# Linear attention inside a mixture-of-experts kernel: transposed quadrant products, reciprocal by Ln and Exp, casting loads, and a new written order for the front

## The chip, the cores and the metric

The kernel runs on one core of a Trainium2 chip. The metric is device time in microseconds (us): 963.81 is the median of three runs of the kernel before. A profiled execution of it gives a trace of every instruction. PE is the matrix engine (TensorE), DVE is VectorE, ACT is ScalarE, POOL is GpSimd and SP is the engine that only issues DMAs.

## The reference

```python
# q, k, v: (8, 8, 576, 64) float32; phi(x) = elu(x) + 1
q_p, k_p = phi(q), phi(k)
kv  = einsum('bhsd,bhse->bhde', k_p, v)
z   = sum(k_p, axis=s)
num = einsum('bhsd,bhde->bhse', q_p, kv)
den = einsum('bhsd,bhd->bhs', q_p, z)[..., None] + 1e-06
x   = (num / den) transposed and reshaped to (4608, 512)
P   = exp(x @ w_gate - max), 8 rounds of row and column normalisation   # (4608, 8)
out = sum over 8 experts e of P[:, e] * (relu(x @ w1[e]) @ w2[e])       # w1: 512x1024, w2: 1024x512
```

Here `phi(x)` is written as min(exp(x), max(x + 1, 1)).

## The kernel before

The work has two stages that overlap. In the first, called the front here, 16 attention steps `att(b, g)` (batch b, four heads g, numbered n = 2b + g) turn q, k and v into the transposed activations `xT` (512 features by 4608 tokens, float16, in SBUF). In the second, 72 units (8 experts by 9 groups g of 512 tokens) each do a first layer and a second layer on PE. The first expert's units run between the attention steps, since unit g of expert 0 needs only the tokens 512g to 512g + 511, so unit 0 needs n = 0 and n = 1. The first five units of expert 0 are plain (`layer1`, L583, then the second layer, L809); all later ones use a seven-product scheme for 2x2 blocks (L703 and L927).

One attention step before: three loads of 576 KB (`kqin`, `vin`, float32, L269), exp of k and q on ACT (L285), max and min on DVE (L298, L301), a cast of v to float16 beside a column of ones (L229 on ACT or L231 on DVE), 18 products of 64 rows for k'v and z (`kv_ps`, L330), a copy that keeps the block diagonal (L341 or L343), nine transposes of q (`qt_ps`, L358), ten products for the denominator (`den_ps`, L373), a reciprocal on DVE (L379, L381), ten products for the numerator (`num_ps`, L397), a multiplication (L402), ten transposes to `xt_ps` (L413) and two copies to `xT`.

The loads of n = 0, 1 and 6 to 15 are issued by SP, those of n = 2 to 5 by POOL. POOL also issues the weights, which are cast from float32 to float16 on the way (L214), in halves for the first expert. At the start PE runs 47 products on zeros (`yw`, L505), which do no work of the kernel.

The order of the instructions on every engine is not the order of the Python loops. Each step is a task of `_Plan` (L18) with an engine, a planned duration, dependences, buffers to acquire and a priority. `run` (L52) goes through the planned time and emits the tasks: each engine takes, of the tasks that could start first, the one with the lowest priority number. A DMA is two tasks: the issue, on `sp` or `pool`, and its transfer, on one planned resource `dma`, which chooses by priority among the transfers already issued:

```python
ti = add(("pool", 1.0), fn, use=[g], prio=prio, deps=[tal, w_part.get(nm) if i else None])
ts_.append(add(("dma", 5.3 / parts), lambda _: None, deps=[ti], use=[g], prio=prio, lat=2.6))
```

The text `ranks` after the units overrides priorities of single tasks, and the engine of some. What is emitted is a fixed order per engine: on the chip an engine waits at each instruction until its operands are there, and does not take a later one first. From unit (1, 0) on the order on PE is fixed by `chain`.

`f_close` (L539) closes the front's buffers after the last attention step and opens those of the seven-product scheme; two products on zeros (`Zye`, L551) mark that place on PE.

Of the kernel before, what the change touches and what calls it, by code (L numbers as in the profile page):

```python
# [122 lines left out]
def kernel(  # L123
# [35 lines left out]
    aps = ctx.enter_context(tc.tile_pool(name="aps", bufs=2, space=PSUM))  # L159
# [5 lines left out]
    xT = xp.tile([P, NDT, N], FP16, tag="xT", name="xT")  # L165
    NXB = 7 * 512
    NL = 4
    NF = 8
    NX = 5
    MG = 99  # L170
# [11 lines left out]
    vv_t = [fp.tile([P, 2, NJ, D + 1], FP16, tag=f"vv{i}", name=f"vv{i}", bufs=1) for i in range(2)]  # L182
    kvps = front.enter_context(tc.tile_pool(name="kvps", bufs=1, space=PSUM))
    diag = fp.tile([P, 2, D + 1], FP16, tag="diag", name="diag", bufs=1)
    half_ = fp.tile([P, 2], FP32, tag="half", name="half", bufs=1)
    p_kv = S_.pool(1)

    p_in = {n: S_.pool(2) for n in "kvq"}
    p_e, p_t = S_.pool(2), S_.pool(2)
    p_vv, p_kvz, p_qpT, p_xn, p_rden = (S_.pool(2) for _ in range(5))  # L190
# [8 lines left out]
    def load_w(ten, nm, pl, ap, cut, e, prio, parts=1, after=0.0, deps=()):  # L199
# [6 lines left out]
        for i in range(parts):  # L206
            def fn(_, i=i):
                dst, a, off = g["tile"], [list(x) for x in ap], e * DM * F
                if parts > 1:
                    n = a[cut][1] // parts  # L210
                    off += i * n * a[cut][0]
                    a[cut][1] = n
                    dst = dst[:, i * n:(i + 1) * n, :] if cut == 1 else dst[:, :, i * n:(i + 1) * n]
                nc.gpsimd.dma_start(out=dst, in_=AP(tensor=ten.tensor, offset=off, ap=a))  # L214
            ti = add(("pool", 1.0), fn, use=[g], prio=prio, deps=[tal, w_part.get(nm) if i else None])
            w_part[nm] = ti
            ts_.append(add(("dma", 5.3 / parts), lambda _: None, deps=[ti], use=[g], prio=prio, lat=2.6))
            w_last[0] = ti
# [20 lines left out]
    v_land, kv_id = [], []  # L239
# [5 lines left out]

    def att(b, g):
# [3 lines left out]
        def ps_home(i):  # L250
            if n < 1 and i < 2:
                return p_ye[i], yps, f"ye{i}"
            return p_att, aps, "att"

        src = [[NJ * D, P], [2 * S * D, 2], [1, NJ * D]]
        gin, tin, gt, tph = {}, {}, {}, {}
        gkq = S_.grp(p_in["k"])
        for nm, ten in (("k", k), ("q", q), ("v", v)):
            gr = gin[nm] = S_.grp(p_in[nm]) if nm == "v" else gkq

            def fn(_, gr=gr, nm=nm, ten=ten):
                if nm == "v":
                    gr["tile"] = fp.tile([P, 2, NJ, D], FP32, tag="vin", name="vin", bufs=2)
                    dst = gr["tile"]
                else:
                    if nm == "k":
                        gr["tile"] = fp.tile([P, 2, 2, NJ, D], FP32, tag="kqin", name="kqin", bufs=2)
                    dst = gr["tile"][:, "kq".index(nm)]
                (nc.gpsimd if 2 <= n <= 5 else nc.sync).dma_start(  # L269
                    out=dst.rearrange("p r j d -> p r (j d)"),  # L270
                    in_=AP(tensor=ten.tensor, offset=(b * H + 4 * g) * S * D, ap=src))
            ti = fadd(("pool", 1.0) if 2 <= n <= 5 else ("sp", 0.45), fn, acq=[] if nm == "q" else [gr],
                      use=[gr] if nm == "q" else [], prio=pr,
                      deps=[w_last[0] if n in (2, 3, 4) else None, in_prev[0]])
            in_prev[0] = ti
            tin[nm] = fadd(("dma", 1.55), lambda _: None, deps=[ti], use=[gr], prio=pr, lat=2.6)
        ge, gtt = S_.grp(p_e), S_.grp(p_t)
        te = []
        for i, nm in enumerate("kq"):
            gt[nm] = gtt  # L280

            def f_e(_, i=i):
                if i == 0:
                    ge["tile"] = fp.tile([P, 2, 2, NJ, D], FP16, tag="e", name="e", bufs=2)
                nc.scalar.activation(out=ge["tile"][:, i], in_=gkq["tile"][:, i], func=AF.Exp)  # L285
            te.append(fadd(("act", 1.17), f_e, deps=[tin[nm], *te], acq=[] if i else [ge], use=[gkq, ge], prio=pr))
        tt_ = None
        for a0, a1 in ((0, 1), (1, 2)) if n < MG else ((0, 2),):
            def tv(g_, a0=a0, a1=a1):
                return g_["tile"][:, :, 2 * a0:2 * a1, :].rearrange("p j r d -> p r j d")  # L290

            def kv_in(g_, a0=a0, a1=a1):
                return g_["tile"][:, a0:a1].rearrange("p a r j d -> p (a r) j d")

            def f_t(_, a0=a0, tv=tv, kv_in=kv_in):
                if a0 == 0:
                    gtt["tile"] = fp.tile([P, NJ, 4, D], FP16, tag="t", name="t")
                nc.vector.tensor_scalar(out=tv(gtt), in0=kv_in(gkq), scalar1=1.0, scalar2=1.0, op0=ALU.add, op1=ALU.max)  # L298

            def f_m(_, tv=tv, kv_in=kv_in):  # L300
                nc.vector.tensor_tensor(out=tv(gtt), in0=tv(gtt), in1=kv_in(ge), op=ALU.min)  # L301
            w = a1 - a0
            tt_ = fadd(("dve", 0.77 if w == 1 else 1.36), f_t, deps=[tin[x] for x in "kq"[a0:a1]] + [tt_],
                       acq=[] if a0 else [gtt], use=[gkq, gtt], prio=pr)
            tm = fadd(("dve", 0.78 if w == 1 else 1.4), f_m, deps=[*te[a0:a1], tt_], use=[ge, gtt], prio=pr)
            for x in "kq"[a0:a1]:
                tph[x] = tm
        gvv = S_.grp(p_vv)
        tvv = []

        def f_va(_):
            gvv["tile"] = vv_t[(len(p_vv["order"]) - 1) % 2]
        ta = fadd(("none", 0.0), f_va, deps=[tin["v"]], acq=[gvv], prio=pr)
        def f_v(e):
            copy(e, gvv["tile"][:, :, :, 0:D], gin["v"]["tile"])
        tvv.append(fadd({"act": 1.15, "dve": 0.76}, f_v, deps=[ta, tin["v"]],
                        use=[gvv, gin["v"]], prio=pr))
        v_land.append(tin["v"])
        if n in (0, 15):
# [5 lines left out]
        def f_kv(_):  # L325
            gkv["tile"] = kvps.tile([P, 2, 512], FP32, tag="kv", name="kv_ps")
            for j in range(NJ):
                for hh in range(2):
                    s = slice(64 * hh, 64 * hh + 64)
                    nc.tensor.matmul(gkv["tile"][:, hh, 0:2 * (D + 1)].rearrange("p (r d) -> p r d", r=2),  # L330
                                     lhsT=gt["k"]["tile"][s, j, 0:2, :].rearrange("p r d -> p (r d)"),
                                     rhs=gvv["tile"][s, :, j, :], start=(j == 0), stop=(j == NJ - 1))
        kv_id.append(len(S_.t))
        tkv = fadd(("pe", 0.54), f_kv, deps=[tph["k"]] + tvv, acq=[gkv], use=[gvv, gt["k"]], prio=pr)

        def f_z(e):
            gz["tile"] = fp.tile([P, 2, 2, D + 1], FP16, tag="kvz", name="kvz")
            kv_ = gkv["tile"][:, :, 0:2 * (D + 1)].rearrange("p h (r d) -> p h r d", r=2)
            if e == "act":
                for r in range(2):  # L340
                    nc.scalar.mul(out=gz["tile"][:, :, r, :], in_=kv_[:, :, r, :], mul=half_[:, r:r + 1])  # L341
            else:
                nc.vector.tensor_tensor(out=gz["tile"], in0=kv_,  # L343
                                        in1=diag[:, None, :, :].broadcast_to([P, 2, 2, D + 1]), op=ALU.mult)
        tz = [fadd({"dve": 0.42, "act": 0.63}, f_z, deps=[tkv], acq=[gz], use=[gkv], prio=pr)]
        gq = S_.grp(p_qpT)

        def f_qa(_):
            gq["tile"] = fp.tile([P, 2, NJ, PW], FP16, tag="qpT", name="qpT")
        tqa = fadd(("none", 0.0), f_qa, deps=[tph["q"]], acq=[gq], prio=pr)  # L350
        tq = []
        for j0, j1 in ((0, 5), (5, NJ)):
            gp = S_.grp(p_att)

            def f_qt(_, j0=j0, j1=j1, gp=gp):
                gp["tile"] = aps.tile([P, 5, 2, PW], FP16, tag="att", name="qt_ps")
                for j in range(j0, j1):
                    nc.tensor.transpose(gp["tile"][:, j - j0, :, :].rearrange("p h w -> p (h w)"),  # L358
                                        gt["q"]["tile"][:, j, 2:4, :].rearrange("p r d -> p (r d)"), ident)

            def f_qc(e, j0=j0, j1=j1, gp=gp):
                copy(e, gq["tile"][:, :, j0:j1, :].rearrange("p h j w -> p j h w"), gp["tile"][:, 0:j1 - j0])
            t1 = fadd(("pe", 0.06 * (j1 - j0)), f_qt, deps=[tph["q"], tqa], acq=[gp], use=[gt["q"]], prio=pr)
            tq.append(fadd({"act": 0.165 + 0.105 * (j1 - j0), "dve": 0.14 + 0.069 * (j1 - j0)}, f_qc, deps=[t1, tqa],
# [836 lines left out]
```

## Time and profile before

| | us |
|---|---|
| runs of the kernel | 962.03, 963.81, 964.0 (median 963.81) |
| span of the profiled execution, first to last instruction | 960.4 |
| PE busy in it | 954.2 (99%) |
| DVE busy | 773.4 (81%) |
| ACT busy | 572.4 (60%) |
| POOL busy | 114.1 (12%) |

The median is 3.4 us above the span; the time around the span in that one execution is not recorded apart. The table counts a matmul as busy until its modelled end, and the products on zeros as busy too, so 99% does not mean that PE worked usefully all that time. The columns of the views below: in a chain, start, length and what it was; in a timeline, start, length, engine, source line, operation and tiles; in a group row, the count after x, then busy time and mean of one.

### The profile page before, as it was taken

How to read it: one execution, taken by the hardware profiler on the slowest of the kernel's cores; microseconds unless marked ns; L12 is line 12 of the kernel's file. 1: busy time of each engine (PE TensorE's matmuls, PEld its weight loads, DVE VectorE, ACT ScalarE, POOL GpSimd, SP SyncE). 2: the span in 40 equal slices, each digit the busy share in tenths (PEclk: the TensorE clock that was granted, in tenths of full speed). 3: DMA queues.
4: the chain of work that ended last, by engine and by line, in shares of the span. 5: the costliest groups of instructions: out<-in, count | busy, mean ns of one | idle time of the engine just before them, and what ended most of it. 6: DMA issues, size and time to landing. Idle time of an engine off the chain costs nothing.

```text
span 960.4 us, 21585 instructions
## 1 busy us (share of the span) xinstructions
PE 954.2 (99%) x8833; PEld 803.7 (84%) x8833; DVE 773.4 (81%) x1527; ACT 572.4 (60%) x1034; POOL 114.1 (12%) x163
## 2 busy tenths in 40 slices
PE   9999999999999999999999999999999999999998
PEld 4666676688888888888888888888888888888886
DVE  6998889878887888878887888878887888877775
ACT  6897755855555555555555555555555555555553
POOL 4100000011111111111111100111111111111110
PEclk9999999999999999999999999999999999999999
DMA  9987962252227222452227222272226321235554
GB/s 317 345 315 259 277 195 77 44 122 78 78 77 165 78 77 78 113 130 77 78 78 164 79 78 78 81 162 74 68 71 136 93 78 74 78 100 164 166 162 114
DMA packets 46420, 121.99 MB, mean 127 GB/s; under 512 B 4208, under 2 KB 18288, under 8 KB 46320
## 3 DMA queue, kind: packets, MB, share of 16 engines
q1 hardware_dynamic: 30576, 96.22, 30.1%
q0 software_dynamic: 15344, 23.87, 12.9%
q8 instruction: 69, 1.13, 0.5%
q10 hardware_dynamic: 400, 0.52, 0.2%
q14 instruction: 31, 0.25, 0.1%
HBM read 119.69 MB, written 17.69 MB: 143 GB/s over the span
## 4 chain that ended last, share of the span: by engine, by line
PE 95%; DMA 2%; ACT 2%; DVE 0%; issue 0%; POOL 0%; ACTq 0%; DVEq 0%
PE ye L927 34%; PE hq L703 24%; PE att L703 12%; PE ye L809 7%; PE Zye L703 6%; PE Zye L927 6%; PE hq L583 3%; DMA kqin<-in_k_dram 2%; ACT e L285 1%; PE xt_ps L413 1%; PE kv_ps L330 1%; PE num_ps L397 1%; PE qt_ps L358 1%; ACT h L587 0%; PE lg_ps L432 0%; PE den_ps L373 0%
## 5 line engine op out<-in xcount | busy, mean ns | idle before, releaser
L941 DVE SCALAR_TENSOR_TENSOR acc<-ye,P_sb,acc 128x256 f32<-128x256 f32 x620 | 267.3, 479 | 128.1 <-PE ye L927 127.6
L703 PEld LDWEIGHTS <-W 128*128 128x128 f16 x2144 | 209.8, 98 | 26.8 <-issue 0.2
L927 PEld LDWEIGHTS <-S 128*128 128x128 f16 x1984 | 194.1, 98 | 22.5
L927 PE MATMUL ye<-T,S 128*128 128x256 f16 x1488 | 192.8, 273 | 0.0
L703 PEld LDWEIGHTS <-w 128*128 128x128 f16 x1608 | 157.4, 98 | 20.1 <-issue 0.7
L735 ACT ACTIVATE h<-hq 128x512 f16<-128x512 f32 x134 | 80.1, 597 | 146.2 <-PE hq L703 143.3
L951 POOL TENSOR_TENSOR acc<-acc,st 128x256 f32<-128x256 f32 x124 | 87.3, 724 | 619.9 <-ACT st L948 609.2
L927 PEld LDWEIGHTS <-h 128*128 128x128 f16 x1488 | 145.6, 98 | 16.8
L703 PE MATMUL att<-xs,W 128*128 128x256 f16 x1008 | 151.2, 273 | 0.0
L703 PE MATMUL hq<-xs,W 128*128 128x256 f16 x1008 | 151.2, 273 | 0.0
L703 PE MATMUL hq<-xs,w 128*128 128x256 f16 x1008 | 140.9, 273 | 0.3 <-DVE h L738 0.3
L732 ACT ACTIVATE h<-Zye 128x512 f16<-128x512 f32 x134 | 80.1, 598 | 42.6 <-PE Zye L703 42.6
L948 ACT ACTIVATE st<-Zye,P_sb 128x256 f32<-128x256 f32 x124 | 51.9, 470 | 78.0 <-PE Zye L927 78.0
L900 DVE TENSOR_TENSOR S<-h 128x1024 f16<-128x1024 f16 x124 | 85.4, 689 | 13.7 <-ACT h L735 13.7
L738 DVE CUSTOM_DVE_ANT_0 h<-att,s 128x512 f16<-128x512 f32 x126 | 86.7, 688 | 11.7 <-ACT s L722 11.1
L722 ACT COPY s<-hq 128x512 f32<-128x512 f32 x126 | 73.6, 584 | 36.3 <-PE hq L703 36.3
L715 ACT COPY Zye<-hq 128x512 f32<-128x512 f32 x134 | 78.0, 582 | 17.8 <-PE hq L703 17.7
L738 DVE CUSTOM_DVE_ANT_0 h<-hq,s 128x512 f16<-128x512 f32 x126 | 86.7, 688 | 0.6 <-PE hq L703 0.6
L809 PE MATMUL ye<-w,h 128*128 128x512 f16 x312 | 76.6, 379 | 0.0
L703 PE MATMUL Zye<-xs,w 128*128 128x256 f16 x504 | 75.6, 273 | 0.0
L729 ACT COPY s<-att 128x512 f32<-128x512 f32 x126 | 74.6, 592 | 0.0
L927 PE MATMUL ye<-w,h 128*128 128x256 f16 x496 | 64.3, 273 | 0.0
(109 smaller groups left out, 949.7 us busy)
## 6 DMA issues: line engine op xcount, KB each, us to landing
xs<-xd SPq DMA_DIRECT2D x63, 896.0 KB, 4.6
w<-in_moe_w_dram POOLq DMA_DIRECT2D x14, 1024.0 KB, 11.5
out_dram<-acc SPq DMA_DIRECT2D x67, 128.0 KB, 2.4
kqin<-in_k_dram SPq DMA_DIRECT2D x12, 576.0 KB, 5.2
kqin<-in_q_dram SPq DMA_DIRECT2D x12, 576.0 KB, 6.6
vin<-in_v_dram SPq DMA_DIRECT2D x12, 576.0 KB, 7.3
xd<-acc SPq DMA_DIRECT2D x5, 512.0 KB, 4.9
kqin<-in_k_dram POOLq DMA_DIRECT2D x4, 576.0 KB, 10.5
```

The source lines that it names most:

```text
L703: nc.tensor.matmul(dst[:, p, :], lhsT=lhs(p, c), rhs=rhs(c), start=(first and p == 0 and c == 0), stop=(c == 1), skip_group_check=True)
L715: nc.scalar.copy(out=Zt[1], in_=gX["tile"])
L722: nc.scalar.copy(out=gs2["tile"], in_=gX["tile"])
L729: nc.scalar.copy(out=gs5["tile"], in_=gR["tile"])
L732: nc.scalar.activation(out=hd(0, 0), in_=Zt[1], func=AF.Relu)
L735: nc.scalar.activation(out=hd(1, 0), in_=gX["tile"], func=AF.Relu)
L738: nc.vector._custom_dve(TENSOR_ADD_SAT, out=dst, in0=ps, in1=sb, s0=3.0e38, s1=0.0)
L809: nc.tensor.matmul(gy[tt]["tile"], lhsT=gh["tile"][:, f, ds(P * tt, P)], rhs=gw2["tile"][:, f, :], start=(f == 0), stop=(f == NFT - 1))
L900: nc.vector.tensor_tensor(out=Sx[:, i], in0=a0, in1=a1, op=op)
L927: nc.tensor.matmul(bank(g_)[:, s, :], lhsT=lhs(s, kk), rhs=rhs(kk), start=(new and s == 0 and kk == 0), stop=(kk == 3), skip_group_check=True)
L941: nc.vector.scalar_tensor_tensor(out=dst(), in0=bank(g_)[:, s, :], scalar=P_sb[:, gg, e:e + 1], in1=dst(), op0=ALU.mult, op1=ALU.add)
L951: nc.gpsimd.tensor_tensor(out=dst(), in0=dst(), in1=gst["tile"], op=ALU.add)
```

## The change

The attention step is written anew, the loads are cast, and the order of the front is another.

1. q and v are loaded as float16 (`qin`, and `vv` with its ones column set once), k as float32 (`kin`), each with three buffers. All loads but the first k are issued by POOL, in one fixed sequence with the first expert's weights: n = 0, n = 1, both halves of w1, the first half of w2, n = 2, the second half of w2, n = 3, and so on. The weights no longer wait for the landing of the first v.
2. q is transposed before phi: 18 transposes of 128x64 blocks (L333 in the new file) into `at2`, one PSUM tile of two banks. Then exp on ACT (L337) and max and min on DVE (L340, L343) on the transposed q.
3. k'v has 192 columns (ones shared by two heads, L308). Numerator and denominator are made transposed, by 64x64 products over 288 tokens (`quads`, L359); the denominator is repeated over 64 rows by a broadcast operand.
4. 1/den is Exp(-Ln(den + 1e-6)) on ACT (L372 twice, L377). A multiplication on DVE writes `xT` (L387), so that the transposes of x and their copies are gone. The numerator uses the PSUM bank of `kv`.
5. The relu of `layer1` may go to ACT or DVE. The bank that was `aps` with two buffers is `at2` for all its users.
6. `ranks` is replaced by `order`, a new list of ranks for the tasks of the front.

```diff
-    vv_t = [fp.tile([P, 2, NJ, D + 1], FP16, tag=f"vv{i}", name=f"vv{i}", bufs=1) for i in range(2)]
+    vv_t = [fp.tile([P, 3, NJ, D], FP16, tag=f"vv{i}", name=f"vv{i}", bufs=1) for i in range(NV)]
...
-            ti = add(("pool", 1.0), fn, use=[g], prio=prio, deps=[tal, w_part.get(nm) if i else None])
+            ti = add(("pool", 0.85), fn, use=[g], prio=prio, deps=[tal, w_part.get(nm) if i else None] + ([in_prev[0]] if e == 0 else []))
+            if e == 0:
+                in_prev[0] = ti
+                if i == 0 and mid:
+                    mid()
...
+        def quads(dst, c, z):
+            for hh in range(2):
+                for r in range(2):
+                    s, o = slice(64 * r, 64 * r + 64), 64 * hh
+                    w = gz["tile"][s, hh, D * (1 - r):D * (1 - r) + 1].broadcast_to([64, D]) if z else gz["tile"][s, hh, r:r + D]
+                    nc.tensor.matmul(dst[o:o + 64, r, 0:CH], lhsT=w,
+                                     rhs=gq["tile"][s, hh, :, :].rearrange("p j w -> p (j w)")[:, CH * c:CH * c + CH],
+                                     start=True, stop=True)
...
+            t1 = fadd(("pe", 0.2), f_den, deps=[tq, *tz], acq=gd, use=[gq, gz], prio=pr)
+            tl.append(fadd(("act", 0.75), f_ln, deps=[t1, *tl], acq=[] if c else [grd], use=[*gd, grd], prio=pr))
+
+        def f_ex(_):
+            nc.scalar.activation(out=grd["tile"], in_=grd["tile"], func=AF.Exp, scale=-1.0)
...
+                nc.vector.tensor_tensor(out=xT[:, 2 * g:2 * g + 2, S * b + CH * c:S * b + CH * c + CH],
+                                        in0=gn["tile"][:, :, 0:CH], in1=grd["tile"][:, c], op=ALU.mult)
...
-    w_t = {0: load_w1(0, prio=-290.0, parts=2, deps=[gates[0]])}
-    for b in range(1, B):
+    w_t = {0: load_w1(0, prio=-290.0, parts=2)}
+    w_t[0] += load_w2(0, prio=-98.5, parts=2, mid=lambda: att(1, 0))
+    att(1, 1)
+    for b in range(2, B):
         att(b, 0)
         att(b, 1)
-        if b == 1:
-            w_t[0] += load_w2(0, prio=-96.5, parts=2, deps=[in_prev[0]])
...
-    ranks = """
+    order = """
...
-    for w in ranks.split():
-        n, p, *en = w.split(":")
+    for i, w in enumerate(order.split()):
+        n, *en = w.split(":")
         t = S_.t[int(n)]
-        t["prio"] = float(p)
-        if en and en[0] in t["eng"]:
+        t["prio"] = 0.1 * i - 2000.0
+        if en:
             t["eng"] = {en[0]: t["eng"][en[0]]}
```

The order that comes out of this for the first microseconds, engine by engine (the numbers of the attention steps are read from the loads' source offsets): POOL issues q0, v0, k1, q1, v1, w1 in two halves, half of w2, k2, q2, v2, the rest of w2, k3, q3, v3, k4, q4, v4. ACT does exp(k0), exp(q0), exp(q1), exp(k1), the two Ln and the Exp of n = 0, the two Ln of n = 1, exp(k3), then the Exp of n = 1 and exp(q3). DVE makes xT of the first half of n = 0, then max and min of k3, then xT of n = 1's first half and of n = 0's second half. PE does the transposes and k'v of n = 0 and 1, their denominators and three of their four numerators, then the transposes of q3, k'v of n = 3, and only then the first eight products of unit 0's first layer (L554).

## The prediction

> **What bounds the kernel now.** I read the busy windows first, then the chain in order of time, then the groups of PE, and last the landings of single loads.
>
> ```profile
> 20.00:34.30 14.30, 14.03 (x136) 7.98 (x136) 12.09 (x24) 10.90 (x17) 4.98 (x7) 1.00 1.15 326
> ...
> 39.30:126.00 86.70, 86.28 (x1010) 54.76 (x1011) 75.51 (x159) 70.62 (x112) 2.09 (x3) 1.00 0.89 285
> ```
>
> The columns are stretch, length, then busy time of PE, weight loads, DVE, ACT and POOL, clock, DMA share, GB/s. From 20 us on PE has almost no idle time; DVE is at 87% and ACT at 81% from 39 to 126. After 193 us PE steps from product to product without a gap. So the time is the end of the start-up plus PE's remaining work, and a microsecond without useful PE work is lost.
>
> The chain shows the start-up:
>
> ```profile
> 0.74 4.30 DMA kqin<-in_k_dram
> ...
> 10.19 9.44 DMA kqin<-in_k_dram
> ...
> 19.71 1.16 ACT e L285
> ...
> 38.67 0.62 PE kv_ps L330 x18
> ...
> 40.56 1.75 PE hq L583 x8
> ...
> 129.05 0.45 PE Zye L551 x2
> ```
>
> The first k lands at 5.04, k2 at 19.63 (10.19 + 9.44). Loads are the limit there. The single issues continue this: v1 issued at 3.53 took 9.0, landing at 12.5; w1's halves issued at 8.54 and 9.46 took 6.3 and 8.0 (14.9, 17.5); v2 issued at 11.97 took 10.7 (22.7); v3 at 14.74 took 12.3 (27.0); the last half of w2, issued at 17.79, took 14.4 (32.2). Landings follow the order of issue, 1.5 us for a load of 576 KB and about 2.5 for half a weight.
>
> What PE did meanwhile, in the groups of PE up to 39.3 us:
>
> ```profile
> L505 PE MATMUL yw<-warm 128*128 128x512 f16 x47 | 14.3, 437 | 1.3 <-DVE warm L493 1.3
> L583 PE MATMUL hq<-xT,w 128*128 128x512 f16 x32 | 7.9, 378 | 0.1
> L809 PE MATMUL ye<-w,h 128*128 128x512 f16 x28 | 7.2, 378 | 0.0
> ...
> L330 PE MATMUL kv_ps<-vv,t 64*128 64x130 f16 x90 | 3.5, 217 | 0.2 <-ACT vv L229 0.2
> L413 PE MATMUL xt_ps<-ident,xn 128*128 128x128 f16 x40 | 3.2, 219 | 0.0
> ```
>
> In the chain four 512-column products step in 0.86 us, so 32 + 28 are 12.9 us; five k'v groups at 0.62, 38 transposes of q and 40 of x at 0.06, 40 numerators at 0.058, 40 denominators at 0.025 add 3.1 + 4.7 + 2.3 + 1.0. Useful work by 39.3: about 24.0 us.
>
> **The change, start-up.** The new sequence of loads is k0, q0, v0, k1, q1, v1, w1, w1, half of w2, n = 2, half of w2, n = 3. That is what landed by 32.2 before (six loads, four halves, six loads), in another order. With v1 at 12.5 as before, three halves bring 20.1, n = 2 24.6, the last half 27.2, then k3 28.7 to 29.2, q3 1.5 later, v3 at 31.7 to 32.2. The casts of q and v are priced by the weights: float32 read at 1 MB in 2.5 us gives 1.4 to 1.5 for 576 KB. POOL's issues take 0.7 to 1.1 us each, less than a landing, and its waits (eight transfers outstanding, buffers of n = 0 and 1) end well before the queue runs dry.
>
> The instructions do not follow that order. ACT has exp(k3) ahead of the Exp of n = 1, DVE has max and min of k3 ahead of two of the first xT halves, and PE has the transposes of q3 and k'v of n = 3 ahead of layer 1 of unit 0, which itself needs neither. n = 2, landed seven microseconds earlier, comes later in all three. So everything waits for k3 and then v3. By hand: n = 0 and 1 are done by about 20 us but for the Exp of n = 1 and three multiplications. k3 at 29.2; exp(k3) to 30.4 (1.18); Exp of n = 1 to 31.6; xT of n = 1, first half, to 32.4 (0.75: the 512-element row of L402 is 0.69, its 256-element row 0.42); numerator and xT of n = 0, second half, to 33.4; k'v of n = 3, waiting for that bank and for v3, to 34.4. Layer 1 starts at 34.4, where before it began at 17.13 with two products and at 19.95 in bulk.
>
> Its first eight products end at 36.1. The next need the last half of n = 1, and DVE has before it exp(q3)'s partner max at 34.5 (exp(q3) ends at 34.45, and max waits for it), then six more of about 0.75, 0.75, 0.27, 0.74, 0.75, 0.74 and 0.75: 39.3. PE's useful work by 39.3 is then: three k'v at 0.92, three sets of q transposes at 0.61, ten groups of quadrant products at 0.18 (all three priced below) and eight layer-1 products, 1.7: 8.1 us. **Deficit 24.0 - 8.1 = 15.9 us.**
>
> **Attention on PE.** Before, one step costs 0.62 (k'v) + 0.61 (transposes of q) + 0.25 (den) + 0.58 (num) + 0.63 (transposes of x) = 2.69. After: k'v has 192 columns for 130; 0.62 x 192/130 = 0.92. The 18 products of 130 columns in 0.62 are 0.034 each, where full-height ones of 130 columns would be 0.055 (215 ns for 512), so 64-row products do run two side by side. For the 64-column half-width of the new transposes no row exists: 18 at half of 0.068 is 0.61, one after another 1.22. Sixteen quadrant products of 288 columns (0.121 each): four side by side 0.18 a group with its start, two side by side 0.24 or more. I take four, as rows of 64 already pair: 0.92 + 0.61 + 0.72 = 2.25, **a saving of 0.44 x 16 = 7.0 us**. Two side by side and serial transposes: 0.92 + 1.22 + 1.0 = 3.14, a loss of 7. Best case 0.75 + 0.5 + 0.55 = 1.8, a saving of 14.
>
> The Trainium skill, page "TensorEngine Tiling (Array Packing)", sections "Key Properties" and "Restrictions", speaks against this: a change of tiling mode drains the array, and column tiling gives up the fast weight load. In the trace the k'v groups, a mode of their own amid full-size products, show no drain that stands out in their 0.62 us; for columns no run here shows it.
>
> **Clock.** The first products on zeros start every 0.43 us up to 6.0 us, then 0.21, although the clock column says 1.00. PE now has little to do from 20 to 32 us, so it may be slow again: k'v of n = 3 on the path would cost 0.9 more, and what follows 39.3 up to the 2.3 that the first slow stretch lost (1.33 to 6.0 at half speed). I take 1.5, of 0 to 3. The page "TensorE: Matmul & The Clock Gate", Part 1, has the clock halve after an idle window of about 3.4 us and return after as much work; by that one such stretch would lose an estimated 1.7 us at most, and the sum would stand 0.2 higher.
>
> **ACT and DVE.** Before, one step is 11.5 us of both (exp 2.36, max and min 3.0, cast 1.1, kvz 0.6, copies 2.2, reciprocal 0.45, multiplication 1.8). After: exp of k 1.18, of q 1.17, two Ln 1.3, Exp 1.18, max and min 1.5 + 1.5, kvz 0.54, two multiplications 1.5: 9.9. Ln has no row; I price it as a 576-element copy from PSUM on ACT (0.65 in L229), between 0.6 and 0.9. The 1.6 x 16 = 25 us off two engines hide behind PE. But those engines stand idle from 20 to 29. From 29.2 on about 141 of attention, 25 of relus, 12 of second-layer copies and 8 of x blocks remain: 186 over two engines, 93 at full use, 111 at the 84% of the second window above. So the front closes between 122 and 140, while PE would need 39.3 + 70 (five plain units) - 1.7 + 16 x 2.25 - 6.4 + 3 = 140. They are close: 2 us of extra idle time, of -2 to +6. POOL adds to it: v5 is issued behind the release of v2's buffer, at about 47.
>
> **Everything else.** The relu on either engine and the ones column are free at this load. The steady units keep their order; the one PSUM tile adds a wait of PE for DVE ahead of one product group in 61 units. Before, that DVE step ends at 507.69 and the group starts at 507.92; a hop from DVE to PE takes 0.06, so 0.17 us covers it. Without that cover each 0.1 us would cost 6.
>
> **Sum.** +15.9 - 7.0 + 1.5 + 2 = +12.4. On the span: 972.8; on the median, 3.4 above the span: 976.2, taken as 976. With each term at its good end (14 saved, no clock loss, idle -2, v3 half a microsecond early) it is -1; at its bad end +15.9 + 7 + 3 + 6 = +32.
>
> **Rivals.** *Quadrants or half-width transposes run in pairs at best:* 3.14 a step, +27, about 990. For it: no row with 64 columns. Against: 64-row pairs do overlap.
> *PE saves more and the lighter ACT and DVE close gaps:* 1.85 a step saves 13.4, and with no extra idle time +15.9 - 13.4 + 1.5 = +4, about 968.
> *Not slower: v3 lands early.* If transfers of this all-POOL sequence overtake one another as the plan's ranks have it, layer 1 starts up to 13 us sooner, at about 21.5, bound by n = 1. Each microsecond earlier than 32.2 pays one; the break-even is v3 at about 20, and with v3 at 17 the whole is 12.4 - 12.9 - 1.5 (clock) - 2 (the second wait) = -4, 960. Against it: k2 behind both halves of w1, landing after them, and every later load in order of issue.
> *The steady units lose their 0.17 us of cover:* +6 or more on top, 982 and up.
>
> **How the numbers follow.** Forecast 0.62; pairs only 0.18; larger saving 0.12; early landing 0.05; steady units 0.03. The range 966 to 988 takes the forecast with its terms, the larger saving and the lower part of the pairs. About 0.2% (1.9 us) is what can be told from no change; faster by more is the early landing alone, 0.05, within it 0.03, slower 0.92.
>
> **What would show it.** Right: k3 landing near 29 and v3 near 32; exp(k3) as the longest wait of ACT, some 9 us; the first eight L554 products near 34 and the next near 39; the two products on zeros at the front's end near 140 for 129.05; from there on the distance to the end unchanged at 831 us. Wrong: L554 near 21, a quadrant group of 0.3 us or more, or the units after 200 us longer than 12.2 us.

## The result and the profile after

The changed kernel takes 990.25 us (median of 4 runs, 989.43 to 991.04) where the kernel before, on the same chip, took 963.9: a ratio of 1.0272, with a 95% interval of 1.0257 to 1.0287. The profiled execution has a span of 987.7 us. The sign of the forecast holds; the loss is 26 us where 12 were forecast, and 990 lies above the range.

The busy windows of the changed kernel (stretch, length, busy PE, weight loads, DVE, ACT, POOL, granted clock, DMA share, GB/s):

```profile
20.00:34.30 14.30, 3.29 (x41) 2.30 (x41) 3.04 (x4) 3.74 (x4) 4.35 (x6) 0.61 1.17 258
34.30:39.30 5.00, 4.13 (x29) 1.62 (x24) 4.75 (x8) 3.46 (x6) 0.00 (x0) 0.75 0.88 192
39.30:126.00 86.70, 82.18 (x838) 39.63 (x838) 60.32 (x99) 65.17 (x93) 23.36 (x31) 1.00 0.74 176
```

PE, which was busy for 14.03 of the first stretch, now is for 3.29, at a granted clock of 0.61. And from 39.3 on, where PE was to work almost without a break, it has 82.18 of 86.70, with *less* work on DVE and ACT than before.

The landing of k3 in the chain, the timeline of PE at the end of the start-up, and what was waited for from 18 to 60 us (total, times, longest):

```profile
13.01 15.61 DMA kin<-in_k_dram
28.61 0.02 issue
28.63 1.16 ACT ek L284
```

```profile
31.69 0.46 PE L359 MATMUL num_ps<-qpT,kvz 64*64 64x288 f16 x4 [11.01 <-DVE xT L387]
32.08 1.17 PE L333 MATMUL att<-ident,qin 128*64 128x128 f16 x18
33.19 1.62 PE L308 MATMUL kv_ps<-vv,t 64*128 64x192 f16 x18
34.74 2.89 PE L554 MATMUL hq<-xT,w 128*128 128x512 f16 x8
...
39.18 0.59 PE L554 MATMUL hq<-xT,w 128*128 128x512 f16 x2
```

```profile
POOL vv L272 <- PE kv_ps L308: 15.2, 1, 15.2
PE num_ps L359 <- DVE xT L387: 11.0, 1, 11.0
DVE t L288 <- DMA kin<-in_k_dram: 9.1, 1, 9.1
ACT ek L284 <- DMA kin<-in_k_dram: 8.1, 1, 8.1
```

This is the start-up that was traced by hand: ACT and DVE at k3, PE behind DVE, layer 1 at 34.74 and again at 39.18.

**Where PE's time went.** I sum, in both traces, from the start of each product to the start of the next. The plain step of its shape (215.5 ns for 512 columns, 109 for 256, in a row of small products what they take in the row) is work; if the tile shape changes between two products, up to 0.1 us of the excess is put down to that; the rest is waiting.

| us | zeros | work | changes of shape (number) | waiting | sum | close of the front |
|---|---|---|---|---|---|---|
| before | 13.0 | 933.8 | 2.9 (31) | 5.4 | 955.0 | 128.91 |
| after | 25.5 | 925.3 | 12.5 (130) | 18.8 | 982.1 | 153.42 |
| difference | +12.5 | -8.5 | +9.6 | +13.4 | +27.1 | +24.5 |

The numbers are rounded. The close is the start of the first product on zeros of `Zye`, here before and after (the 129.05 of the prediction is its place in the chain):

```profile
128.91 0.59 PE L551 MATMUL Zye<-warm 128*128 128x512 f16 x2
153.42 0.59 PE L522 MATMUL Zye<-warm 128*128 128x512 f16 x2
```

The column of zeros takes in what passes between a product on zeros and the next start: its +12.5 is for the most part PE standing idle up to 31.69, behind the last of these products. Of the waiting, 2.6 us lie between 31.7 and 39.3 (about 1 of them is the slow clock on the first eight products of layer 1), 9.0 between 39.3 and the close (before: 1.3), and 3.4 more than before after the close, around the column sums of the Sinkhorn rounds, for a reason that no run shows; later the units stand as before.

A change of shape can be read in the timeline, where four 512-column products ahead of quadrants take 0.95 us to the next start (56.68 to 57.63) and not 0.86:

```profile
56.68 1.02 PE L782 MATMUL ye<-w,h 128*128 128x512 f16 x4
57.63 0.32 PE L359 MATMUL num_ps<-qpT,kvz 64*64 64x288 f16 x4
57.88 1.90 PE L782 MATMUL ye<-w,h 128*128 128x512 f16 x8
```

Single starts say the same: 309 ns from a 512-column product to a quadrant, a 128x64 transpose or a k'v product, and about 0.1 us on the way back (239 ns from the start of a group's last quadrant to a 512-column product, 137 to the next group of quadrants). In the trace before only k'v did this (312 ns); transposes, numerators and denominators had full-size tiles and cost nothing (215 ns).

The waits of DVE after 39 us, and the chain there, show a second thing that the change brought:

```profile
DVE qpT L340 <- ACT eq L337: 14.0, 12, 2.4
```

```profile
45.63 1.14 ACT eq L337
...
46.80 0.77 DVE qpT L340
...
47.61 0.71 PE att L333 x18
48.34 1.14 ACT eq L337
...
49.50 0.77 DVE qpT L340
...
50.31 0.34 PE att L359 x4
50.65 0.02 issue
50.67 0.75 ACT rden L372
```

The max of q (L340) starts when the Exp (L337) has ended, one behind the other on the one PSUM tile `at2`; the denominators and the next step's transposes need that tile too. After 39 us the chain goes through such a pair nine times. Before, exp and max read SBUF and ran beside each other.

### The profile page after: what moved, and what is told of

Read it like the earlier page. It is cut to its first block, busy times and chain, and to the rows that moved or that the text cites. A ratio compares the mean times of both kernels' runs of the same rounds, so it can differ in the third digit from the quotient of the medians.

```text
span 987.7 us, 21380 instructions
## 1 busy us (share of the span) xinstructions
PE 961.1 (97%) x8753; PEld 789.0 (80%) x8753; DVE 765.5 (78%) x1463; ACT 574.1 (58%) x1022; POOL 139.2 (14%) x197
## 4 chain that ended last, share of the span: by engine, by line
PE 89%; DVE 4%; ACT 3%; DMA 2%; issue 1%; POOL 0%; POOLq 0%; ACTq 0%
PE ye L900 33%; PE hq L676 23%; PE att L676 12%; PE Zye L676 6%; PE Zye L900 5%; PE ye L782 5%; PE hq L554 3%; DMA kin<-in_k_dram 2%; ACT eq L337 1%; PE kv_ps L308 1%; PE att L333 1%; DVE qpT L340 1%; DMA vv<-in_v_dram 1%; PE num_ps L359 0%; ACT rden L377 0%
## 5 line engine op out<-in xcount | busy, mean ns | idle before, releaser
L900 PEld LDWEIGHTS <-S 128*128 128x128 f16 x1984 | 194.1, 98 | 22.5
```

The source lines that it names most:

```text
L900: nc.tensor.matmul(bank(g_)[:, s, :], lhsT=lhs(s, kk), rhs=rhs(kk), start=(new and s == 0 and kk == 0), stop=(kk == 3), skip_group_check=True)
```

## Experiments

The kernel before ran again beside each round of experiments, with medians of 963.1 to 964.1 us, so runs of different rounds can be compared to about 1 us.

My first theory was the start-up alone, with the written order as its cause: the plan lets its loads land by priority (k3 ahead of k2 and of half the weights), and the chip lands them as issued.

**The plan serves loads in order of issue (e1); the same without the written list (e2).**

```diff
-                    if r is not None and r <= te + 1e-9 and (pick is None or (t["prio"], t["id"]) < (pick["prio"], pick["id"])):
+                    if r is not None and r <= te + 1e-9 and (pick is None or key(t) < key(pick)):
     # key(t): (ready, id) for the transfers, else (prio, id); in e2 the text `order` is gone too
```

> The plan serves its loads in the order in which POOL issues them, as the chip did (k2 landed at 21.81, k3 at 28.61); the written list of ranks stays. Theory 'start-up only': the 26 us are the instructions that wait for n = 3; in the new order on PE both groups n = 0 and 1 and ten layer-1 products come ahead of anything of n = 2 and 3, so layer 1 starts near 21 for 34.74, the products on zeros keep PE from 20 to 31.7 no longer, and the front closes 24 us sooner, near 130; time about 965. Theory 'start-up and shape changes': layer 1 near 21 too, but only the first part comes back, 11.6 us of idle time and 3.8 of waits before 39.3; the 130 changes of tile shape (12.5 us) stay and the close is near 140; time about 976. Rival 'the list itself is at odds with the landings': ranks that were found for other landings give their gain back later, layer 1 near 21 and yet the close at 150 or later; time 985 or more.

> As the last one, and the written list is left out: every step has the rank of its group n, the lower first. Layer 1 needs n = 0 and 1 alone (v1 landed at 12.35) and starts near 20. Theory 'start-up only': close near 130 to 135, time 965 to 970. Theory 'start-up and shape changes': shape changes are as many as before (117 in the front, 0.095 us each), so close near 140, time 975 to 978. Rival 'the list is what costs': this one beats the kernel that keeps the list by 5 us or more. Rival 'nothing in the order matters': within 2 us of 990.

Measured: 1028.43 and 1000.34, both slower than 990. Layer 1 starts at 22.47 and 20.93 as expected, and the idle stretch is gone; but the close comes at 179.6 and 150.6, and PE's waiting is about 67 and 38 us. So a start-up that is 12 us shorter can be worth less than nothing: the rest of the front has to fit as well. "Start-up only" fell, and the rivals that put the cost on the written list held: with the right landings the plan is 28 us faster without it. But e2 too is 10 us slower than the changed kernel. I did not follow every wait in these two.

**The price of a change of shape, alone (z1, z2).**

```diff
                         nc.tensor.matmul(bank(g_)[:, s, :], lhsT=lhs(s, kk), rhs=rhs(kk),
                                          start=(new and s == 0 and kk == 0), stop=(kk == 3), skip_group_check=True)
+                        if s == 0 and kk == 1:   # z1: r = c = 128; z2: r = c = 64
+                            nc.tensor.matmul(bank(g_)[0:c, s, :], lhsT=warm[0:r, 0:c], rhs=warm[0:r, 0:256],
+                                             start=False, stop=False, skip_group_check=True)
```

> Measures the disputed cost by itself, in the steady units, where PE steps without a gap: after the second of the eight products of each of 434 groups one more product of 128x128 on zeros is added to the same bank (256 columns, adds nothing). Both theories: 434 x 0.109 us = 47 us on top, about 1037.

> As z1_full, but the product on zeros has 64 rows and 64 columns, so 434 x 2 changes of tile shape. Theory 'a change of shape costs 0.095 us each way' (309 ns where a plain step is 215, 239 where four quadrants take about 137): 47 + 868 x 0.095 = 47 + 82 = 130 us on top, about 1120. Rival 'the gaps at the quadrants are waits for other engines, not the shape': as z1_full within 5 us, about 1037, or less, since a quadrant loads less weight. Rival 'the array drains, but only when the products before wait for the quadrant's result': no cost here either.

Measured: 1038.46 and 1133.01, so 48 and 143 us on top (one run each, against 990.25). The quadrant costs 94.6 us more than the full product, 0.218 us for a change there and back. The timeline of z2:

```profile
400.51 0.38 PE L900 MATMUL ye<-w,S 128*128 128x256 f16 x2
400.82 0.29 PE L903 MATMUL ye<-warm 64*64 64x256 f16 x1
401.05 0.39 PE L900 MATMUL ye<-w,S 128*128 128x256 f16 x2
```

Start to start it is 202 ns into the quadrant and 226 out of it, where z1 has 109 both times. Nothing waits for another engine here. The price is real, about 0.1 us each way, and both rivals fell. The weight loads of the same stretch show what is held up:

```profile
400.29 0.32 PEld L900 LDWEIGHTS <-S 128*128 128x128 f16 x3
400.82 0.10 PEld L903 LDWEIGHTS <-warm 64*64 64x64 f16 x1 [0.21 <-issue]
401.04 0.55 PEld L900 LDWEIGHTS <-S 128*128 128x128 f16 x6
```

In the row a load starts with the product before its own, 0.1 us ahead; at all 434 insertions the quadrant's load, and the first one behind it, start only with their own products (here at 400.82 and 401.04). The load itself is hardly longer (103 ns for 98). Whether PE waits there for the array to empty or for the weights, these records do not tell apart.

**The loads in the order that the plan had assumed (r1), a deeper v (r2), both (r3).** Here the emitted order of PE, ACT, DVE and SP is kept instruction by instruction; in r1 only POOL's issues move.

```diff
     # tasks of q0 v0 q1 k1 v1, half of w1, k3 q3 v3 k2 k4 v4, half of w1, q4 q2 v2, w2 in halves
+    first = [38, 40, 65, 63, 67, 91, 127, 129, 131, 97, 154, 158, 93, 156, 99, 101, 96, 125]
+    loads = first + [x for x in full if x not in first]
...
+    seq = sorted(S_.seq, key=lambda x: at.get(x[0]["id"], pos[x[0]["id"]]))
-    NV, NK, NQ = 3, 3, 3
+    NV, NK, NQ = 4, 3, 3      # r2 and r3
```

> Every instruction of PE, ACT, DVE and SP in the order of the changed kernel; POOL alone issues the first loads in another order, the one in which the plan had them land: q0 v0 q1 k1 v1, first half of w1, k3 q3 v3, k2 k4 v4, second half of w1, q4 q2 v2, w2. From v1 at 12.35, at 1.45 us for a load and 2.5 for half a weight, k3 lands at 16.4, v3 at 19.3, the last half of w2 at 35.5. Theory 'the order of the instructions was written for other landings': layer 1 comes 6.1 us after k3 as before (28.61 to 34.74), at 22.5; the idle stretch from 20 to 31.7 goes and 11 to 12 us of it stay gained: time 978, close of the front near 141. Rival 'given back': n = 2 and w2, now later, stop PE again; layer 1 at 22.5, close within 3 us of 153, time 987 to 990. Rival 'all waits of the front have this one origin, and changes of shape cost nothing': close near 130, time 965 to 968.

> The changed kernel with four buffers for v instead of three, all orders kept: v5 no longer waits on POOL for k'v of n = 2 (15.2 us there, issued at 49.5), and the loads behind it are issued earlier. Theory 'holes in the loads stop PE': of the 9 us of PE's waits from 39 to 153 about half go, time 985 to 986. Rival 'PE does not wait for loads there' (after 39 us the only wait of ACT, DVE or PE for a load of the front is 0.7 us): within 1 us of 990.

> Both edits. If the first alone gains 12 us, the loads are needed 12 us earlier, and v's buffers may bind: theory 'the holes bite once the start-up is short': 2 to 4 us less than the first alone, near 975. Rival: the same as the first alone within 1 us.

Measured: 985.65, 991.04 and 985.54. Layer 1 starts at 26.67 in r1, 8 us sooner (expected at 22.5; k3 landed at 18.76 for 16.4), but only 4.6 us stay: the time lies between the first theory and "given back", nearer the second. The deeper v changes nothing: the 15.2 us wait of POOL is real and nobody needs its loads sooner. The chain of r1 shows where the rest went:

```profile
16.70 8.98 DMA vv<-in_v_dram
...
26.26 13.00 DMA kin<-in_k_dram
...
39.35 1.16 ACT ek L297
```

k5, now behind both halves of w2, lands at 39.26, and exp(k5) stands next on ACT: the wait had moved one load further. So r4 issues k5 right behind the second half of w1.

> As r1_reissue (985.65, close of the front at 150.7), with k5 issued right behind the second half of w1 and not behind w2: in r1 it landed at 39.3, and the chain hung on it for 13 us up to exp(k5). It should land near 29.7. Theory 'what r1 gave back was this load': the 4 to 5 us between the second eight of layer 1 and the close that r1 took longer than the changed kernel come back, time 981, close 146. Rival 'a chain through one PSUM tile sets the pace after the start-up' (transposed q, Exp, max, then the denominators, all in att): 1 us or nothing, 985.

Measured: 981.43, close 146.86, as the theory said. With the instructions of PE, ACT, DVE and SP in the same order as in the changed kernel, the order of the loads alone is worth 8.8 us.

**Nine full transposes for eighteen of half width (q1).**

```diff
-            for j in range(NJ):
-                for r in range(2):
-                    nc.tensor.transpose(at2.rearrange("p a b -> p (a b)").bitcast(FP16)[64 * r:64 * r + 64, P * j:P * j + P],
-                                        gin["q"]["tile"][:, r, j, :], ident)
+            qf = gin["q"]["tile"].rearrange("p r j d -> p (r j d)")
+            for j in range(NJ):
+                nc.tensor.transpose(at2.rearrange("p a b -> p (a b)").bitcast(FP16)[:, P * j:P * j + P], qf[:, P * j:P * j + P], ident)
```

> The changed kernel in its order, but q is transposed by nine products of 128x128 a step for eighteen of 128x64; this leaves out the placing of q's columns (they land in other rows), so only its time means anything. 21 of the 130 changes of tile shape go, and the product time stays (0.53 a step in pairs, 9 x 0.056 = 0.50 in full). Theory 'each change costs PE 0.1 us': 2.1 us less where PE is the limit, near 988. Rival 'the gaps are waits for ACT and DVE, which keep their pace': within 0.5 us of 990.

Measured: 990.91, nothing gained. In its trace the price is gone (216 ns into the transposes, 56 out; 111 changes for 130), but PE's waiting grew from 18.8 to 20.5:

```profile
62.53 1.04 PE L563 MATMUL hq<-xT,w 128*128 128x512 f16 x4
63.41 0.67 PE L343 MATMUL att<-ident,qin 128*128 128x128 f16 x9
63.91 1.03 PE L563 MATMUL hq<-xT,w 128*128 128x512 f16 x4
```

The loads of this execution landed 1.9 us later than in the changed kernel's (k3 at 30.50, layer 1 at 36.60), which could hide a gain. From the start of layer 1 to the close it took 118.2 us for 118.7, so about 0.5 of the 2.1 us came back. PE's own time mostly did not set the end of the front; a loop with ACT and DVE is the likely cause, and the next run tests a part of it.

**The max apart from the Exp (l1), and with r4's loads (l2).**

```diff
-            nc.vector.tensor_scalar(out=gq["tile"], in0=qps(), scalar1=1.0, scalar2=1.0, op0=ALU.add, op1=ALU.max)
+            nc.vector.tensor_scalar(out=gq["tile"], in0=zq, scalar1=1.0, scalar2=1.0, op0=ALU.add, op1=ALU.max)
```

> The changed kernel in its own order of instructions and loads; the max of q reads a tile of zeros in SBUF and not the transposed q in PSUM, so it waits no longer for the Exp that reads the same PSUM tile (DVE waited 14.0 us for it in 12 of 13 steps after 39 us); this leaves q + 1 out of the feature map. Nine times after 39 us the chain runs Exp (1.14) and then max (0.77) before PE goes on. Theory 'this serial pair in the loop of the one PSUM tile costs': 9 x 0.77 = 6.9 us less at most, 4 to 7: time 983 to 986. Rival 'PE's own time sets the end there, with its changes of shape': within 1.5 us of 990.

> r4 and l1 together (q + 1 is left out here too). If the landings and the serial pair are separate costs the gains add: 990 - 9 - 6 = 975. If one covers the other, no better than the better of the two by more than 1 us. What would then be left over 964 is the changes of shape, up to 9.6 us.

Measured: 985.34 and 974.71. The waits of DVE from 39 to 150 us in l1, and its group of the max (count, busy, mean ns, idle before):

```profile
DVE qpT L353 <- ACT eq L347: 2.9, 3, 1.6
```

```profile
L350 DVE TENSOR_SCALAR qpT<-zq 128x1152 f16<-128x1152 f16 x13 | 5.9, 451 | 0.0
```

The max (L350) waits for nothing any more; the 2.9 us left are the min (L353). 4.9 us come back, and from the start of layer 1 to the close 5.1 (113.6 for 118.7); the max itself is shorter too (451 ns for 0.77 us), which I did not separate. With both edits 15.5 us come back, a little more than 8.8 + 4.9; that each loss partly covered the other is my reading and was not tested.

**The full transposes once more, where PE binds (l3).** l2 with q1's edit.

> l2_reissue_max_apart (974.71) with q transposed by nine products of 128x128 a step; this leaves out q + 1 and the placing of q's columns. In q1 the same edit gave nothing (990.91 for 990.25), while the loop of the one PSUM tile and the landings bound the front. Theory 'with these two gone PE's own time binds, and a change of shape costs its 0.1 us': 21 changes less, 2.1 us, 972.6. Rival 'changes of shape are covered in the front in any case': 974.7 within 0.7.

Measured: 973.59, 1.1 us less than l2, between the two theories. The waiting in l2 is still 12.9 us by the sum above, so PE's time binds in part of the front only. How much of the 9.6 us of shape changes lies on the path in the changed kernel itself stays open, between q1's nothing and their full price.

**All work kept, the order made anew (s1, s2), and the same for the kernel before (c1).** The priorities of the front were searched in a plan that lands loads as issued, starts the max after its Exp and charges 0.1 us a change of shape; s2 also copies the transposed q out of PSUM first.

```diff
+        def f_qc(_):      # s2
+            nc.vector.tensor_copy(out=gqc["tile"], in_=qps())
-            nc.scalar.activation(out=geq["tile"], in_=qps(), func=AF.Exp)
+            nc.scalar.activation(out=geq["tile"], in_=gqc["tile"], func=AF.Exp)     # and the max reads gqc too
...
-    S_.run()
+    S_.emit(seq.split())     # the order found, written out
```

> The changed kernel's instructions, all of them, with the front in an order searched once more in a plan that knows three things: loads land in the order of their issue, the max of q starts after its Exp, and a change of tile shape costs PE 0.1 us. Nothing is left out. If the written order's mismatch to the landings was the cause of r4's gain and of more waits besides: 990.2 - 8.8 = 981 or less; with the serial pair still there, up to 7 us of it, not below 970: 972 to 978. Rival 'a search gains nothing over the order of the changed kernel with its loads in place': 981 or more.

> As s1, and DVE first copies the transposed q out of PSUM (0.77 us); the Exp (1.14) and the max (0.45 from SBUF, as l1 shows) then read the copy side by side, and the PSUM tile is free 1.1 us sooner in each step. Nothing is left out. PE's useful work 925.4, zeros 13, changes of shape 12.5, and waits at best the 5.4 of the kernel before: 956.3, where before it was 955.0 for 963.8; so 965 at best, with l2's waits (12.9) and zeros (16.3) 974. Expected 965 to 970. Rival 'the attention in quadrants is slower by its kind': not below 974.

> Control for s1 and s2: the kernel before with all its instructions and its loads in their order of issue, and its front in an order searched in the same plan (loads land as issued, 0.1 us for a change of tile shape). If the search itself makes kernels faster and not the fit to the landings, it gains here too: its waits (5.4 us in all) and changes of shape (2.85) leave at most 5, so 959 to 962. Rival 'the kernel before was in step with its landings already, so there is nothing to regain': 962 to 967, within 0.4% of it.

> s2_copy_first once more, beside the control: 967.4 again, within 1.5 us, 0.3 to 0.5% over the kernel before.

Measured: s1 974.76, s2 967.39 and again 968.06, c1 966.80. Against the kernel before, measured beside them, s2 is at 1.0037 (1.0024 to 1.0050 in its second measurement) and c1 at 1.0025 (1.0015 to 1.0036). The windows of s2:

```profile
20.00:34.30 14.30, 13.64 (x152) 6.76 (x152) 10.21 (x18) 11.36 (x16) 3.63 (x5) 1.00 1.19 248
39.30:126.00 86.70, 86.70 (x948) 41.62 (x940) 75.87 (x128) 72.09 (x102) 22.57 (x31) 1.00 0.94 215
```

PE is busy again from 20 us on at full clock, and the front closes at 129.08 for 128.91 before. By the sum: zeros 14.3, work 924.4, changes of shape 12.1, waiting 7.8, together 958.6 for 955.0. The search gives the kernel before nothing (966.80, slightly worse), so the order of that kernel shows no such loss, and the changed kernel's does. Of the 23 us that s2 regained, r4 puts 8.8 on the order of the loads and l1 4.9 on the max behind the Exp (15.5 together in l2); the rest came with the new order and is not taken apart. No version here beats the kernel before.

## Why the prediction missed

**Landings, order of issue: right.** k3 landed at 28.61 (said 28.7 to 29.2), v3 at 31.40 (31.7 to 32.2), all in order of issue; the rival "v3 lands early" fell.

**Start-up: right.** Layer 1 at 34.74 (said 34.4), the next products at 39.18 (39.3). That the first fits to 0.3 us is partly luck: k3 came 0.6 us sooner than the 29.2 of the working, and k'v of n = 3 took 1.55 us at the slow clock for 0.92. Zeros aside, PE had done 23.2 us of work by 39.3 before and 8.0 now (small rows at the pace that they ran), a deficit of 15.2 for 15.9. r4, which moves loads alone and has layer 1 at 26.96, shows its cause.

**Attention on PE: right, slightly better than said.** Quadrants do run four side by side (starts 2 to 4 ns apart, 0.15 us from one group to the next for the 0.18 taken) and half-width transposes in pairs; PE's work fell by 8.5 us for 7.0. By the pace within its rows a step costs 1.88 us for the 2.25 taken, and the step before 2.41 for 2.69: both were priced too high by about 0.3, so that the saving came out near is partly luck. The rival "pairs only" fell; that its number, about 990, is the time measured is chance, since its cause did not happen.

**Clock: right in kind, not in place.** 0.61 and 0.75 granted; the eight first products took 2.89 us, where eight take 1.90 later (57.88 above). But from 39.3 to 126 the granted clock is 1.00: the slow stretch lies within the start-up, whose deficit holds it already, and none of the 1.5 us came on top.

**Steady units: right.** The product group behind the one PSUM tile waits for nothing (0.1 us of idle time before its 1008 products). The distance from the close to the end is 834.3 for 831.5, by the waiting around the Sinkhorn rounds, which the prediction did not have.

**The failed step: "2 us of extra idle time, of -2 to +6".** From 39.3 on PE loses 20.3 us more than before: 9.2 by changes of shape and 7.7 by waiting up to the close (said near 140, was 153.42), and 3.4 behind it. So the sum of +15.9 - 7.0 + 1.5 + 2 was in the trace +15.2 - 8.5 + 0 + 20.3 = +27.0. These are shares of PE's time, not what each would give back if it alone were taken out. Three things were missing from that term.

- *A change of tile shape.* I had the rule before me, the Trainium skill's "TensorEngine Tiling (Array Packing)", "Key Properties", that a change of tiling mode drains the array, and put it aside since no drain "stands out" in k'v's 0.62 us. It does not stand out there because it lies at the edges of the group: 312 ns to its first product where a 512-column product otherwise steps on in 215, and some 0.1 us behind its last, which the 0.62 already held (the pace within the group makes 0.53). z2 gives 0.218 us there and back. At 99 more changes this was a term of up to 10 us, larger than the saving that I did count; how much of it lay on the path stays open (q1, l3).
- *Exp and max in series on PSUM.* I saw that max(q3) waits for exp(q3) and used it once, in the start-up; it held in 12 of the 13 steps after 39 us. l1 puts 4.9 us on it, with the shorter max; s1 against s2, each with an order of its own, 7.4.
- *ACT and DVE were priced by their sums.* 1.6 us a step less work on two engines that are not full says nothing of a loop from transposes over Exp, max, min and denominators to Ln through one PSUM tile. q1 (2.1 us off PE, about 0.5 back) and l1 point to this loop and not PE's sum as what set the pace; its other links were not tested one by one.

POOL's wait for v5, which I named as an addition, cost nothing (r2).

In s2, with the copy and an order made for the true landings, 9.4 us less work on PE is paid back by 9.2 us of shape changes: in the best version here the change is worth nothing (0.4% slower than the kernel before), and as it was ordered it costs 26 us.

## What to carry to other kernels

Count the changes of tile shape on PE as instructions of their own, here 0.1 us each, before counting what smaller tiles save; read them as starts at the edges of a group, not inside it. When a step moves its operands from SBUF to PSUM, look at who may read that tile at the same time and what else lives in it, and price the loop through it, not the sums of the engines. An order written out in advance is only as good as its model of the queues: move the loads alone, all else kept, and see what comes back.

## What the runs showed of the hardware

- Products of 64x64 on four quadrants start 2 to 4 ns apart, and a group of four with 288 columns follows another in 0.15 us; 128x64 transposes and 64x128 k'v products run in pairs (18 in 0.53 and 0.76 us).
- A change between tile shapes costs PE 0.093 us going into a 64x64 product and 0.117 coming back, even in an unbroken row of products with no other engine to wait for (z2); weights are not loaded ahead across it.
- The landing of q0 varied from 5.96 to 8.33 us between profiled executions and kernels and moved the later loads with it by 1 to 2 us (layer 1 of the changed order at 34.74, 35.73, 36.23 and 36.60). I have no cause for it, and it limits what a single start-up can show.
